# The sums of a sliding-window attention burst: first of 72 small matmuls, or behind 24 of them

## The chip, the core and the metric

The kernel runs on one core of one Trainium2 chip. The metric is the device time of one execution in microseconds (us); where several executions are given, their median counts. A change is measured against runs of the kernel before on the same chip.

## The reference

Two attention blocks read the same input x (2048 rows of 1024) and are mixed by a gate. Block A is linear attention; block B, which the change touches, is a local attention of 32 heads of 32: each position looks at 8 keys, 2 apart, at or before itself.

```python
H = 32; Dh = D // H
W, dil = 8, 2
idx = pos[:, None] - (jnp.arange(W) * dil)[None, :]      # positions looked at
mask = idx >= 0
logits = jnp.einsum("bhsd,bhswd->bhsw", q, kg) * Dh ** -0.5
logits = jnp.where(mask[None, None, :, :], logits, -1e9)
attn = _softmax(logits, axis=-1)
o = jnp.einsum("bhsw,bhswd->bhsd", attn, vg)
b = o_as_rows @ wo
...
return g * a + (1 - g) * b          # g = sigmoid((x * gate_w).sum(-1))
```

The softmax is computed as exponentials of the masked scores, a sum over the keys (the denominator), and a sum of values weighted by the exponentials, divided by the denominator at the end.

## The kernel before

**Stages.** The even and the odd positions are held apart, so that "2 apart" becomes "next to each other". TensorE first makes B's values for all rows (L1405 to L1414), then B's keys and queries (L1507 to L1523), then A's keys, A's state matrix (L1620 to L1643), A's queries and the output (L1688 and on). Each of these is made of groups of 8 or 16 matmuls of 128x128 weights against 512 columns, recorded at L1349, L1628 and L1700.

**The local attention** is cut into 18 fills: 9 for each parity, of 2 x 57 or 2 x 56 queries. They are strewn between the large groups by `slot` (L1493), one fill to five groups or so. A fill (`fill`, L1435) has these operations:

- two DMAs that fetch 2 x 64 rows of values into `vt` (L1441);
- the score burst `s_fn` on TensorE (L1444): 64 small matmuls, 32-row tiles of the array, whose 57 columns each land in the four PSUM banks `SO[0]` to `SO[3]` (banks 4 to 7);
- the exponential on ScalarE into `E` (L1454) and the band mask on VectorE (L1457);
- three slots later (`PVLAG`), the values burst `values` (L1461): in one operation, `each` (L1463), 64 value matmuls and 8 sum matmuls;
- then, for each half, the logarithm of the denominators (L1483), the exponential of its negative (L1484), both on ScalarE, and the product with the weighted values (L1485) on VectorE.

**The values burst.** All 72 matmuls use tiles of 64 rows x 32 columns of the array: the row half h (0 or 1) holds one set of 64 keys, the column quarter j (0 to 3) one of four heads. So there are eight tiles, and the loops over j and h visit them in turn. A value matmul (L1468) has a head's 64 x 32 values as weights and streams 57 columns of E, one head's; it writes `SO[h]`. There are 8 x 4 x 2 = 64, with c from 0 to 7 outermost. A sum matmul (L1474) has a 64 x 32 block of ones as weights and streams 456 columns of E, the eight heads of one j at once; it writes `SO[2 + h]`. There are eight, one on each tile. Every matmul is preceded by a weight load of its own, so the burst is 72 pairs. In the kernel before, the sums stand behind the round c = 2, that is behind 24 value matmuls (`SUMS_AT = 2`, L1251 and L1471).

**What sets the order of the work.** A planner (`Prog`, L63) collects operations with costs and dependencies, lays them out in time by these costs (`schedule`, L122), and `emit` (L207) writes each engine's list. A dependency across engines is a wait on a semaphore ahead of the operation's first instruction; an operation counts its semaphore up once, on the instruction that its function returns, here on `last`, the last value matmul. The order within an operation is that in which its function issues. The planner books the values burst at 0.66 us, whatever stands inside it, and so does not see the order of the 72 pairs.

Of the kernel before, what the change touches and what calls it, by code (L numbers as in the profile page):

```python
# [1119 lines left out]
def build_kernel(nc, A_x, A_wqkv, A_wo, B_x, B_wqkv, B_wo, gate_w, out):  # L1120
# [10 lines left out]
    def SB(shape, dtype, name, at=None):  # L1131
        n = SZ[dtype]
        for d in shape[1:]:
            n *= d
        if at is None:
            at = base[0]
            base[0] += (n + 31) // 32 * 32
        uid[0] += 1
        h = nc.alloc_sbuf_tensor_at("%s_%d" % (name, uid[0]), list(shape), dtype, offset=at)
        return Tile("S", h, at, list(shape), dtype)  # L1140
# [48 lines left out]
    def hb(p0, p1, half):  # L1189
        return [("H%d" % half, p0, p1, None)]  # L1190
# [9 lines left out]
    ones = SB([128, 128], BF16, "ones")  # L1200
# [47 lines left out]

    FILL = 0.2
    PVLAG = 3  # L1250
    SUMS_AT = 2  # L1251
    WARM = 50
    PASSES = 6
    mm = lambda n: max(n / 2400.0, 0.0267) + 0.0025
# [3 lines left out]
    def plan(seen):  # L1258
# [169 lines left out]
        SO = banks[4:8]  # L1428
# [6 lines left out]
        def fill(e_, qs, nq, offs):  # L1435
            t0 = e_ * HS
            k0 = [qs + nq * h - offs[h] for h in range(2)]
            m = msk[KINDS.index((nq, offs))]
            vt, vslot = vr.next()
            for h in range(2):  # L1440
                P.op("sp", lambda e, h=h: e.dma_start(vt[64 * h:64 * h + 64, :], vB_hbm[t0 + k0[h]:t0 + k0[h] + 64, :]), 0.4,  # L1441
                     reads=[hb(t0 + k0[h], t0 + k0[h] + 64, i) for i in range(2)], writes=[vt.all()], chan="v%d_%d" % (vslot, h), lat=0.5)

            def s_fn(e):  # L1444
                for c in range(8):
                    for h in range(2):
                        for j in range(4):
                            last = e.matmul(SO[j].ap(c * nq, (c + 1) * nq)[64 * h:64 * h + 64, :], kT[32 * j:32 * j + 32, c, t0 + k0[h]:t0 + k0[h] + 64],  # L1448
                                            qT[32 * j:32 * j + 32, c, t0 + qs + h * nq:t0 + qs + (h + 1) * nq], start=True, stop=True, tile_position=(32 * j, 64 * h))
                return last  # L1450
            P.op("pe", s_fn, 0.65, mode="r", reads=[kT.part((0, 8), (t0 + k0[0], t0 + k0[1] + 64)), qT.part((0, 8), (t0 + qs, t0 + qs + 2 * nq))],
                 writes=[s.iv for s in SO], name="S")
            E, _ = Er.next()
            P.op("act", lambda e: e.activation(E[:, 0:32 * nq].rearrange("p (j q) -> p j q", j=4), ps[:, 4:8, 0:8 * nq], ACT.Exp), act(32 * nq),  # L1454
                 reads=[s.iv for s in SO], writes=[E.all()])
            ev = lambda: E[:, 0:32 * nq].rearrange("p (g q) -> p g q", g=16)
            mk = P.op("dve", lambda e: e.tensor_tensor(ev(), ev(), m[:, :, :].rearrange("p r q -> p (r q)")[:, None, :].to_broadcast([128, 16, 2 * nq]), ALU.mult),  # L1457
                 0.15 + 32 * nq / 1920.0, reads=[E.all(), m.all()], writes=[E.all()])
            masks.append(mk)

            def values():  # L1461

                def each(e):  # L1463
                    for c in range(8):
                        for j in range(4):
                            for h in range(2):
                                hd = 4 * c + j
                                last = e.matmul(SO[h].ap(c * nq, (c + 1) * nq)[32 * j:32 * j + 32, :], vt[64 * h:64 * h + 64, hd * 32:hd * 32 + 32],  # L1468
                                         E[64 * h:64 * h + 64, (8 * j + c) * nq:(8 * j + c + 1) * nq],
                                         start=True, stop=True, tile_position=(64 * h, 32 * j))  # L1470
                        if c == SUMS_AT:  # L1471
                            for j in range(4):
                                for h in range(2):
                                    e.matmul(SO[2 + h].ap(0, 8 * nq)[32 * j:32 * j + 32, :], ones[64 * h:64 * h + 64, 0:32],  # L1474
                                             E[64 * h:64 * h + 64, 8 * j * nq:8 * (j + 1) * nq],
                                             start=True, stop=True, tile_position=(64 * h, 32 * j))
                    return last
                bi = [s.iv for s in SO]
                P.op("pe", each, 0.66, mode="c", reads=[vt.all(), ones.all(), E.all()], writes=bi, name="PV")
                for g in range(2):  # L1480
                    L, _ = Lr.next()
                    pb = lambda o, g=g: ps[:, 4 + 2 * o:6 + 2 * o, 4 * g * nq:4 * (g + 1) * nq]
                    P.op("act", lambda e, L=L, pb=pb: e.activation(L[:, :, 0:4 * nq], pb(1), ACT.Ln), act(8 * nq), reads=[SO[2].iv, SO[3].iv], writes=[L.all()])  # L1483
                    P.op("act", lambda e, L=L: e.activation(L[:, :, 0:4 * nq], L[:, :, 0:4 * nq], ACT.Exp, scale=-1.0), act(8 * nq), reads=[L.all()], writes=[L.all()])  # L1484
                    P.op("dve", lambda e, L=L, pb=pb, g=g: e.tensor_tensor(  # L1485
                        qT[:, 4 * g:4 * g + 4, t0 + qs:t0 + qs + 2 * nq].rearrange("p c (h q) -> p h c q", h=2),
                        pb(0).rearrange("p h (c q) -> p h c q", c=4), L[:, :, 0:4 * nq].rearrange("p h (c q) -> p h c q", c=4), ALU.mult), dps(8 * nq),
                        reads=[SO[0].iv, SO[1].iv, L.all()], writes=[qT.part((4 * g, 4 * g + 4), (t0 + qs, t0 + qs + 2 * nq))])
            after(PVLAG, values)
# [12 lines left out]
        def after(n, f, cols=False):  # L1502
            later.append((slot_n[0] + n, f, cols))
            later.sort(key=lambda x: x[0])
# [291 lines left out]
def bass_gated_mix__linear_attn_block__sliding_local_dilated__prompt_kernel(nc, A_x, A_wqkv, A_wo, B_x, B_wqkv, B_wo, gate_w, out):  # L1796
    return build_kernel(nc, A_x, A_wqkv, A_wo, B_x, B_wqkv, B_wo, gate_w, out)
# [28 lines left out]
```

## Time and profile before

| | us |
|---|---|
| median of 3 runs | 486.28 (486.14 to 486.35) |
| the profiled execution | 485.35 |
| its span, from the first to the last instruction | 483.5 |
| TensorE matmuls busy | 480.0, 99% |
| VectorE busy | 294.9, 61% |
| ScalarE busy | 146.9, 30% |
| the first values burst, by the chain of work that ended last | 131.24 to 131.96 |

Times inside the profile count from the first instruction. A line such as L1468 is a line of the kernel; PE is TensorE's matmuls and PEld its weight loads, which overlap the matmuls. DVE is VectorE, ACT ScalarE. A timeline row gives the start, the length from the first start to the last end of the instructions that it merges, the engine, line, operation, what is written and read, the tile of the array (64*32), the operand's shape, and the count. Square brackets hold idle time ahead, and who ended it. Matmuls on different tiles overlap, and each lasts longer than its columns stream. The granted TensorE clock was full (1.0) over the whole span.

### The profile page before, as it was taken

The page shows a single profiled execution, that of the slowest core. Times are in us where ns is not written, and L with a number is a line of the kernel's source. Part 1 is how long each engine was busy: PE and PEld are TensorE (multiplying, and loading weights), DVE is VectorE, ACT ScalarE, POOL GpSimd, SP SyncE. Part 2 cuts the span into 40 slices and gives each one's busy share as a digit, 9 for nine tenths or more (in the row PEclk, how much of TensorE's full clock was granted, in tenths as well). Part 3 has the DMA queues.
Part 4 walks back from the last instruction along what each step waited for, and adds up shares of the span by engine and source line. Part 5 has one row for each costly group of instructions (what it writes and reads, how often), then busy time and mean ns, then how long its engine had stood idle before and what let it go on. Part 6 is the DMA issues. An engine that isn't in the chain of part 4 may idle for free.

```text
span 483.5 us, 10963 instructions
## 1 busy us (share of the span) xinstructions
PE 480.0 (99%) x4882; PEld 229.0 (47%) x4882; DVE 294.9 (61%) x490; ACT 146.9 (30%) x229; POOL 39.4 (8%) x40
## 2 busy tenths in 40 slices
PE   9999999999999999999999999999999999999997
PEld 6444444444444444444455555444444444444444
DVE  2212186799777778766733222489987777767522
ACT  2111111112344446666654356264222000011000
POOL 3000000000000000000015757010000000000000
DMA  8999996223100032013004340571234111122111
GB/s 243 203 190 322 340 342 188 81 94 107 26 23 26 25 110 73 27 34 111 24 25 122 129 104 4 132 197 24 65 89 87 45 43 45 44 66 66 45 45 48
DMA packets 73977, 48.51 MB, mean 100 GB/s; under 512 B 38337, under 2 KB 67394, under 8 KB 73922
## 3 DMA queue, kind: packets, MB, share of 16 engines
q1 hardware_dynamic: 73090, 46.94, 35.5%
q10 hardware_dynamic: 832, 0.79, 0.8%
q8 instruction: 40, 0.66, 0.6%
q14 instruction: 15, 0.12, 0.1%
HBM read 30.41 MB, written 8.39 MB: 80 GB/s over the span
## 4 chain that ended last, share of the span: by engine, by line
PE 99%; DVE 0%; issue 0%
PE ps_all L1349 58%; PE ps_all L1700 23%; PE ps_all L1628 12%; PE ps_all L1448 2%; PE ps_all L1468 2%; PE ps_all L1385 1%; PE ps_all L1474 1%; PE ps_all L1607 1%; PE ps_all L1655 0%; DVE o L1379 0%
## 5 line engine op out<-in xcount | busy, mean ns | idle before, releaser
L1349 PE MATMUL ps_all<-w,xT 128*128 128x512 bf16 x512 | 112.9, 379 | 0.0
L1349 PE MATMUL ps_all<-xT,w 128*128 128x512 bf16 x512 | 112.2, 379 | 0.0
L1349 PEld LDWEIGHTS ps_all<-xT,w 128*128 128x128 bf16 x512 | 49.3, 98 | 58.7
L1349 PEld LDWEIGHTS ps_all<-w,xT 128*128 128x128 bf16 x512 | 49.0, 98 | 57.6
L1355 ACT ACTIVATE e<-ps_all 128x512 bf16<-128x512 f32 x64 | 38.2, 597 | 109.5 <-PE ps_all L1349 108.7
L1700 PE MATMUL ps_all<-w,qT 128*128 128x512 bf16 (+1 forms) x264 | 60.7, 373 | 0.0
L1700 PE MATMUL ps_all<-kT,aT 128*128 128x512 bf16 (+1 forms) x264 | 60.7, 373 | 0.0
L1349 PE MATMUL ps_all<-kT,xT 128*128 128x512 bf16 x256 | 57.9, 379 | 0.0
L1628 PE MATMUL ps_all<-pk,xn 128*128 128x512 bf16 x256 | 57.8, 380 | 0.0
L1700 PEld LDWEIGHTS ps_all<-w,qT 128*128 128x128 bf16 x264 | 25.8, 98 | 29.6 <-issue 0.2
L1700 PEld LDWEIGHTS ps_all<-kT,aT 128*128 128x128 bf16 x264 | 25.8, 98 | 29.4
L1349 PEld LDWEIGHTS ps_all<-kT,xT 128*128 128x128 bf16 x256 | 24.7, 98 | 30.0 <-issue 0.7
L1376 DVE CAST vst<-ps_all 128x512 bf16<-128x512 f32 x16 | 11.1, 692 | 45.4 <-PE ps_all L1349 45.4
L1628 PEld LDWEIGHTS ps_all<-pk,xn 128*128 128x128 bf16 x256 | 23.9, 98 | 27.4
L1379 DVE TENSOR_SCALAR o<-ps_all,gm 128x512 bf16<-128x512 f32 (+1 forms) x27 | 19.7, 731 | 28.0 <-PE ps_all L1700 28.0
L1356 DVE TENSOR_SCALAR e<-e 128x512 bf16<-128x512 bf16 x64 | 18.8, 296 | 27.5 <-ACT e L1355 27.2
L1454 ACT ACTIVATE E<-ps_all 128x1824 bf16<-128x1824 f32 (+1 forms) x18 | 30.4, 1688 | 15.8 <-PE ps_all L1448 15.1
L1457 DVE TENSOR_TENSOR E<-E,msk 128x1824 bf16<-128x1824 bf16 (+1 forms) x18 | 19.8, 1103 | 23.3 <-ACT E L1454 23.3
L1590 POOL TENSOR_TENSOR zacc<-zacc,pk 128x1024 f32<-128x1024 f32 x15 | 32.0, 2130 | 16.5 <-DVE E L1457 15.7
L1485 DVE TENSOR_TENSOR qT<-ps_all,L 128x456 bf16<-128x456 f32 (+1 forms) x36 | 21.2, 625 | 19.4 <-ACT L L1484 19.2
L1377 ACT ACTIVATE kT<-ps_all 128x512 bf16<-128x512 f32 x25 | 14.2, 599 | 33.6 <-PE ps_all L1349 33.6
L1377 ACT ACTIVATE vst<-ps_all 128x512 bf16<-128x512 f32 x16 | 9.6, 597 | 48.7 <-PE ps_all L1349 48.7
(63 smaller groups left out, 361.0 us busy)
## 6 DMA issues: line engine op xcount, KB each, us to landing
v<-vB_hbm SPq DMA_DIRECT2D x36, 128.0 KB, 2.6
vB_hbm<-vst SPq DMA_DIRECT2D x32, 128.0 KB, 4.9
w<-in_B_wqkv_dram SPq DMA_DIRECT2D x4, 1024.0 KB, 8.4
xt<-in_A_x_dram SPq DMA_DIRECT2D x16, 256.0 KB, 5.3
w<-in_A_wqkv_dram SPq DMA_DIRECT2D x4, 1024.0 KB, 9.7
xn<-in_A_x_dram SPq DMA_DIRECT2D x8, 512.0 KB, 3.7
out_dram<-o SPq DMA_DIRECT2D x15, 256.0 KB, 2.1
kT<-in_A_wqkv_dram SPq DMA_DIRECT2D x2, 1024.0 KB, 5.6
```

The source lines that it names most:

```text
L1349: last = e.matmul(bank.ap(), lhs(dc), rhs(dc), start=(dc == 0), stop=(dc == 7))
L1355: P.op("act", lambda e: e.activation(e_[:, :], bank.ap(), ACT.Exp), act(512), reads=[bank.iv], writes=[e_.all()])
L1356: P.op("dve", lambda e: e.tensor_scalar(e_[:, :], e_[:, :], 1.0, 1e-6, op0=ALU.min, op1=ALU.add), 0.25, reads=[e_.all()], writes=[e_.all()])
L1376: fd = lambda e: e.tensor_copy(dst, src())
L1377: fa = lambda e: e.activation(dst, src(), ACT.Copy)
L1379: fd = lambda e: e.tensor_scalar(dst, src(), scale, None, op0=ALU.mult)
L1454: P.op("act", lambda e: e.activation(E[:, 0:32 * nq].rearrange("p (j q) -> p j q", j=4), ps[:, 4:8, 0:8 * nq], ACT.Exp), act(32 * nq), rea ...
L1457: mk = P.op("dve", lambda e: e.tensor_tensor(ev(), ev(), m[:, :, :].rearrange("p r q -> p (r q)")[:, None, :].to_broadcast([128, 16, 2 * n ...
L1485: P.op("dve", lambda e, L=L, pb=pb, g=g: e.tensor_tensor(qT[:, 4 * g:4 * g + 4, t0 + qs:t0 + qs + 2 * nq].rearrange("p c (h q) -> p h c q" ...
L1590: P.op("pool", lambda e, t=t: e.tensor_tensor(zacc[:, :], zacc[:, :], pkS[:, t, :], ALU.add), 2.2, reads=[src, zacc.all()], writes=[zacc.a ...
L1628: last = e.matmul(bank.ap(), tl[:, t, cs:cs + 128], pkS[:, t, r * 512:(r + 1) * 512], start=(t == 0), stop=(t == NT - 1))
L1700: last = e.matmul(bank.ap(0, f1 - f0), lh[:, k, t * 128:(t + 1) * 128], w[:, k, f0:f1], start=(first and k == 0), stop=(not first and k == 7))
```

## The change

The loop with the eight sums is moved from behind the round c = 2 to the front of `each`, and the constant that named the place goes. Operands, shapes, tile positions, the number of instructions, the operation's reads and writes and its booked cost stay as they are.

```diff
-    SUMS_AT = 2
...
                 def each(e):
+                    for j in range(4):
+                        for h in range(2):
+                            e.matmul(SO[2 + h].ap(0, 8 * nq)[32 * j:32 * j + 32, :], ones[64 * h:64 * h + 64, 0:32],
+                                     E[64 * h:64 * h + 64, 8 * j * nq:8 * (j + 1) * nq],
+                                     start=True, stop=True, tile_position=(64 * h, 32 * j))
                     for c in range(8):
                         for j in range(4):
                             for h in range(2):
...
                                 last = e.matmul(SO[h].ap(c * nq, (c + 1) * nq)[32 * j:32 * j + 32, :], vt[64 * h:64 * h + 64, hd * 32:hd * 32 + 32],
...
-                        if c == SUMS_AT:
-                            for j in range(4):
-                                for h in range(2):
-                                    e.matmul(SO[2 + h].ap(0, 8 * nq)[32 * j:32 * j + 32, :], ones[64 * h:64 * h + 64, 0:32],
-                                             E[64 * h:64 * h + 64, 8 * j * nq:8 * (j + 1) * nq],
-                                             start=True, stop=True, tile_position=(64 * h, 32 * j))
                     return last
```

## The prediction

> **What bounds the kernel now.** The page comes first: which engine is full, and whether the chain that ends last ever leaves it.
>
> ```profile
> span 483.5 us, 10963 instructions
> PE 480.0 (99%) x4882; PEld 229.0 (47%) x4882; DVE 294.9 (61%) x490; ACT 146.9 (30%) x229; POOL 39.4 (8%) x40
> ...
> PE 99%; DVE 0%; issue 0%
> PE ps_all L1349 58%; PE ps_all L1700 23%; PE ps_all L1628 12%; PE ps_all L1448 2%; PE ps_all L1468 2%; PE ps_all L1385 1%; PE ps_all L1474 1%; PE ps_all L1607 1%; PE ps_all L1655 0%; DVE o L1379 0%
> ```
>
> TensorE is the whole path, so whatever a values burst gains or loses on TensorE is gained or lost in the span. The next view is the chain in order of time around one burst, then the two lines' own groups (duration in ns, min/median/max).
>
> ```profile
> 125.95 5.29 PE ps_all L1349 x24
> 131.24 0.21 PE ps_all L1468 x24
> 131.44 0.19 PE ps_all L1474 x8
> 131.64 0.33 PE ps_all L1468 x40
> 131.96 5.29 PE ps_all L1349 x24
> ```
> ```profile
> L1468 PE MATMUL ps_all<-E,v x1152: 182/194/198, 131.2 to 314.3; 64*32 64x57 bf16 x172, 64*32 64x56 bf16 x20
> L1474 PE MATMUL ps_all<-E,ones x144: 347/350/352, 131.3 to 313.9; 64*32 64x456 bf16 x128, 64*32 64x448 bf16 x16
> ```
>
> A burst is 24 value matmuls, 8 sums, 40 value matmuls, 0.72 us in all, and there are 144 / 8 = 18 bursts. The chain dates pieces by ends, so what limits the burst has to be read from its starts. The timeline of the first burst, weight loads (PEld) and matmuls apart, cut where the loads pause:
>
> ```profile
> 131.16 0.17 PEld L1468 LDWEIGHTS ps_all<-E,v 64*32 64x32 bf16 x24 [0.42 <-DVE mx L1308]
> 131.24 0.11 PEld L1474 LDWEIGHTS ps_all<-E,ones 64*32 64x32 bf16 x8
> 131.29 0.09 PEld L1468 LDWEIGHTS ps_all<-E,v 64*32 64x32 bf16 x1
> 131.16 0.28 PE L1468 MATMUL ps_all<-E,v 64*32 64x57 bf16 x24
> 131.26 0.37 PE L1474 MATMUL ps_all<-E,ones 64*32 64x456 bf16 x8
> ...
> 131.39 0.28 PEld L1468 LDWEIGHTS ps_all<-E,v 64*32 64x32 bf16 x24
> ...
> 131.65 0.21 PEld L1468 LDWEIGHTS ps_all<-E,v 64*32 64x32 bf16 x15
> 131.89 0.10 PEld L1349 LDWEIGHTS ps_all<-xT,w 128*128 128x128 bf16 x1
> ```
>
> Second figure: from the first start to the last end; one load lasts 0.09. So 24 + 8 + 1 = 33 loads and 24 + 8 = 32 matmuls, 65 instructions, start between 131.16 and 131.29, at about 3 ns a pair of load and matmul... and then no load for 0.10 us. From 131.39 loads come steadily: 24 in 0.28 - 0.09 = 0.19 us, 8.3 ns each. The 24th starts at 131.58, and a second hold follows: the next starts at 131.65, 0.06 later instead of 0.008. Fifteen more at the same pace start up to 131.65 + 0.21 - 0.09 = 131.77, and 0.12 later the next group loads. The **pace and the holds of the issue**, not the array, set this burst from 131.29 to 131.77, two thirds of its 0.72 us.
>
> What ends a hold? I look at the single first matmul of the values burst, and of the score burst (L1448), which has 64 small matmuls and no sums:
>
> ```profile
> 131.16 0.20 PE L1468 MATMUL ps_all<-E,v 64*32 64x57 bf16 x1
> ```
> ```profile
> 125.25 0.21 PE L1448 MATMUL ps_all<-qT,kT 32*64 32x57 bf16 x1
> ...
> 125.25 0.23 PEld L1448 LDWEIGHTS ps_all<-qT,kT 32*64 32x64 bf16 x33 [0.42 <-issue]
> ...
> 125.49 0.35 PEld L1448 LDWEIGHTS ps_all<-qT,kT 32*64 32x64 bf16 x31
> 125.88 0.10 PEld L1349 LDWEIGHTS ps_all<-xT,w 128*128 128x128 bf16 x1
> ```
>
> Values: the first matmul ends at 131.16 + 0.20 = 131.36, and load 34 starts 0.03 later. Scores: it ends at 125.25 + 0.21 = 125.46, and load 34 starts 0.03 later, again after exactly 33 loads. The second hold of the values: the 25th matmul is the first sum, 131.26 + 0.35 = 131.61, and the 58th load starts at 131.65, 0.03 to 0.04 later; that is again 65 instructions behind it (matmul 25 is instruction 50, load 58 is instruction 115). The score burst has no long matmul, and its last 31 loads run unbroken: 30 x 8.3 ns + 0.10 = 0.35. The last values burst, 183 us later, does the same (first matmul, then load 34):
>
> ```profile
> 313.74 0.20 PE L1468 MATMUL ps_all<-E,v 64*32 64x56 bf16 x1
> ...
> 313.97 0.09 PEld L1468 LDWEIGHTS ps_all<-E,v 64*32 64x32 bf16 x1
> ```
>
> 313.74 + 0.20 + 0.03 = 313.97. My reading: **at most 65 instructions are under way, and a later one enters 0.03 us after the end of the matmul 65 places ahead**. Every burst starts with a full stock because the group before it takes 5.29 us for 24 matmuls, 0.22 each.
>
> **The change part by part.** Nothing is added or taken away: 72 pairs before and after, the same operands, one count at the end of the operation, the same cost in the planner's books, hence the same order of all operations. No DMA is issued in the burst and nothing passes another queue. Only the place of 8 pairs moves, 24 places ahead, 18 times. Four things follow.
>
> 1. The array. The eight sums now start at 131.16 to 131.19 and stream together for 0.19 (chain row), to 131.36. The 25 pairs behind them that are already under way run then: three rounds of eight took 131.16 to 131.26, 0.10, so they are through by about 131.46. In the kernel before, the sums streamed from 131.26 to 131.45, and the first hold (131.29 to 131.39) lay wholly beside them. That cover goes: the array runs empty behind 131.46 until load 34 arrives.
>
> 2. The first hold. Load 34 waits for the first matmul, which is now a sum. How long does a sum at the head of a burst last? The trace shows none there. Lower end: 0.35, its median in the middle. Upper end: 0.36. The first value matmul lasts 0.20 (198 ns is the maximum of L1468), while the 24th, started just ahead of 131.26 and ended at 131.16 + 0.28 = 131.44, lasts 0.19; so the head costs about 0.01 more. I take 0.36, because the nearest row is the first matmul of this very burst. Load 34 then starts at 131.16 + 0.36 + 0.03 = 131.55 instead of 131.39: 0.36 - 0.20 = **0.16 us later**.
>
> 3. The second hold. Matmul 25 becomes a value matmul, started by 131.46, ended by 131.65; by step 2's pace load 58 comes at 131.55 + 24 x 0.0083 = 131.75, later than 131.65 + 0.03 = 131.68. So the hold of 0.06 becomes a plain 0.008: **0.05 us back**.
>
> 4. The tail. From load 34 to load 72 are 38 steps of 8.3 ns, 0.317: the last load starts at 131.55 + 0.317 = 131.87, against 131.77; in hundredths that is 0.10, by the two holds 0.16 - 0.05 = 0.11, and I keep the latter, since it has fewer rounded ends. The 0.12 to the next group stays; behind the score burst, whose last load starts at 125.49 + 0.25 = 125.74, it is 0.14 without any sum in the burst. It is how a change from small tiles to whole-array weights looks, and the last matmuls are value matmuls in both kernels.
>
> Sum per burst: 0.11 us later. Times 18: **+2.0 us**; with 0.35 for the sum, 0.10 and +1.8. Nothing late on another engine follows: who waits for the burst is the logarithm, and it waits for the last value matmul, not for the sums:
>
> ```profile
> ACT L L1483 <- PE ps_all L1468: 14.5, 18, 2.9
> ```
>
> The operation counts once, on its last instruction, so earlier sums let nobody start earlier; and ACT and DVE, 30% and 61% busy, follow TensorE, which waits for them nowhere in the chain. They are 0.11 late with it, as is every later transfer.
>
> The profiled execution took 485.35 us (its span of 483.5 and 1.85 around it), 0.9 below the median of 486.28. The sum is made on the span: 483.5 + 2.0 = 485.5, so a profiled execution of 487.35. On the median: 486.28 + 2.0 = **488.3 us**.
>
> [...]
>
> **The rivals.** *Issue does not wait for ends: faster.* Place freed at the start of an instruction, or new ones after a fixed time. Load 34 then stays at 131.39, no second hold is left, and the last load comes at 131.39 + 0.317 = 131.71, by the one hold 0.05 earlier: 18 x 0.05 = 0.9 us, 485.4. It decides below a load 34 of 131.44, 0.28 behind the start of the burst. For it: the first hold alone shows only 0.20 against 0.21 of matmul time. Against it: these 0.01 do come back in load 34 (0.23 and 0.24 behind the start), and the second hold has no cause without the first sum's end. 6%.
>
> *The second hold is no sum's.* If it belongs to the place in the code, at the 58th pair, it stays: 0.16 a burst, 18 x 0.16 = 2.9 us, 489.2. For it: it stands at load 58 in every burst I read. Against: the score burst passes its 58th load unbroken. 6%.
>
> *Nothing changes.* If the next group's first load were bound to something older than the last value matmul, such as a wait of its own at 131.89, up to 0.12 of lateness would vanish there: 486.3. Against: the score burst, of another length, shows the same distance of 0.14 behind its last load. 5%. That the edit does nothing to the order is excluded: it moves instructions within one operation.
>
> **How the numbers follow.** Forecast 83%, rivals 6, 6 and 5%. About 0.2%, 1.0 us, is what a measurement of this kernel can tell from no change. Slower by more: the forecast and the second rival, 89%. The first rival's 0.9 us lies just inside the bound, so I split it 2% faster and 4% same; with the 5% of no change that makes 9% same. Range: the forecast's ends, 0.10 and 0.11 a burst, give 488.1 to 488.3; an uncertain pace and drain of 0.02 a burst adds 0.4 to either side, and the medians' own spread of 0.1 stands beside it: 487.6 to 488.8. That holds the forecast's 83% and reaches to no rival.
>
> **What would show it.** In the timeline of the changed kernel: eight sums first, at the start of the burst; their first lasts 0.36; 33 loads, then a hold that ends 0.39 behind the start (right), or 0.23 (first rival). After it 39 loads unbroken at 8.3 ns (right), or broken by 0.06 at the 58th (second rival). The next group's load 0.12 behind the last (right). In the chain, a values burst of 0.83 instead of 0.72, everything else as before. Wrong would be above all a first sum that ends sooner at the head of a burst, or a sequencer that refills while the sums stream.

## The result and the profile after

The change makes the kernel slower: median 488.01 us (487.62 to 488.68, 6 runs) against 486.21 us (485.49 to 486.45, 6 runs) of the kernel before, a ratio of 1.0045 with a 95% interval of 1.0033 to 1.0057. On 486.2 that is 1.6 to 2.8 us, and 2.0 was forecast. The profiled execution took 487.88 us.

In the code after, the sums stand at L1465 and the values at L1472; other lines move up by one or two. The page:

```profile
span 486.1 us, 10898 instructions
PE 475.3 (98%) x4817; PEld 230.0 (47%) x4882; DVE 295.0 (61%) x490; ACT 146.9 (30%) x229; POOL 39.4 (8%) x40
...
PE 98%; issue 2%; DVE 0%
```

TensorE still is the whole path. The new 2% of "issue" is no idle time: there are 4882 weight loads and only 4817 matmuls, so 65 records of matmuls are missing in this trace. In the chain a large group shows 5.13 us for 23 matmuls behind 0.16 of "issue", together the 5.29 that 24 took before. The chain around the second burst:

```profile
143.80 0.32 PE ps_all L1465 x8
144.12 0.52 PE ps_all L1472 x64
144.64 0.16 issue
144.80 5.13 PE ps_all L1348 x23
```

A burst now counts 0.32 + 0.52 = 0.84 us instead of 0.72. Where the 0.12 lie is seen in the timeline of the first burst (start, length, count), loads first:

```profile
131.69 0.11 PEld L1465 LDWEIGHTS ps_all<-E,ones 64*32 64x32 bf16 x8 [0.42 <-DVE mx L1307]
131.72 0.33 PEld L1472 LDWEIGHTS ps_all<-E,v 64*32 64x32 bf16 x25
...
132.09 0.41 PEld L1472 LDWEIGHTS ps_all<-E,v 64*32 64x32 bf16 x39
132.53 0.10 PEld L1348 LDWEIGHTS ps_all<-xT,w 128*128 128x128 bf16 x1
...
131.69 0.39 PE L1465 MATMUL ps_all<-E,ones 64*32 64x456 bf16 x8
131.89 0.27 PE L1472 MATMUL ps_all<-E,v 64*32 64x57 bf16 x24
```

Again 8 + 25 = 33 loads and 8 + 24 = 32 matmuls, then no new load until 132.09, which is 0.40 behind the start of the burst; before it was 0.23. Then 39 loads run unbroken: 0.41 - 0.09 = 0.32 us for 38 steps of 8.3 ns. The 24th value matmul starts at 131.89 + 0.27 - 0.19 = 131.97, so from then on the array has nothing to start for 0.1 us. The sums' own row has the length that the forecast had to guess (ns, min/median/max):

```profile
L1465 PE MATMUL ps_all<-E,ones x144: 359/363/363, 131.7 to 316.3; 64*32 64x456 bf16 x128, 64*32 64x448 bf16 x16
```

131.69 + 0.36 + 0.03 = 132.08 to 132.09: load 34 again enters 0.03 behind the end of the first matmul. The last burst agrees, 0.39 from its start at 316.23 (its sums have 448 columns) to load 34:

```profile
316.23 0.11 PEld L1465 LDWEIGHTS ps_all<-E,ones 64*32 64x32 bf16 x8 [0.42 <-issue]
316.26 0.32 PEld L1472 LDWEIGHTS ps_all<-E,v 64*32 64x32 bf16 x25
...
316.62 0.41 PEld L1472 LDWEIGHTS ps_all<-E,v 64*32 64x32 bf16 x39
```

Below, "burst" means from its first weight load to the next group's first weight load, as a mean over the 18 bursts of a trace: 0.724 us before, 0.839 after. The difference times 18 is 2.08 us. The two profiled spans differ by 2.6, and the rest stands ahead of every burst. The warm-up matmuls of the first rows, before and then after:

```profile
0.84 5.33 PE ps_all L1385 x50
```
```profile
0.84 5.86 PE ps_all L1384 x50
```

0.53 us more until the first real group may start. Two kernels below, with the sums behind 32 and behind 40 values, differ from the one before in a single constant and show 5.30 and 5.83 here, so it is a difference between executions and not the change's.

### The profile page after: what moved, and what is told of

Its sections match the earlier page's. It is cut to its first block, busy times and chain, and to the rows that moved or that the text cites. A ratio compares the mean times of both kernels' runs of the same rounds, so it can differ in the third digit from the quotient of the medians.

```text
span 486.1 us, 10898 instructions
## 1 busy us (share of the span) xinstructions
PE 475.3 (98%) x4817; PEld 230.0 (47%) x4882; DVE 295.0 (61%) x490; ACT 146.9 (30%) x229; POOL 39.4 (8%) x40
## 4 chain that ended last, share of the span: by engine, by line
PE 98%; issue 2%; DVE 0%
PE ps_all L1348 56%; PE ps_all L1698 23%; PE ps_all L1626 11%; PE ps_all L1447 2%; PE ps_all L1472 2%; PE ps_all L1384 1%; PE ps_all L1465 1%; PE ps_all L1605 1%; PE ps_all L1653 0%; DVE o L1378 0%
## 5 line engine op out<-in xcount | busy, mean ns | idle before, releaser
L1348 PE MATMUL ps_all<-w,xT 128*128 128x512 bf16 x493 | 109.5, 379 | 2.4 <-issue 2.1
L1348 PE MATMUL ps_all<-xT,w 128*128 128x512 bf16 x497 | 109.9, 379 | 1.7 <-issue 1.4
L1626 PE MATMUL ps_all<-pk,xn 128*128 128x512 bf16 x242 | 54.9, 379 | 2.1 <-issue 2.1
```

The lines of the kernel that those rows point to most:

```text
L1348: last = e.matmul(bank.ap(), lhs(dc), rhs(dc), start=(dc == 0), stop=(dc == 7))
L1626: last = e.matmul(bank.ap(), tl[:, t, cs:cs + 128], pkS[:, t, r * 512:(r + 1) * 512], start=(t == 0), stop=(t == NT - 1))
```

## The experiments

Theory, as in the prediction, where it is the author's reading of the rows before: at most 65 instructions are under way; the next one enters 0.03 us after the end of the matmul 65 places ahead. In all 18 bursts of the trace before, load 34 starts 0.030 to 0.031 us behind the recorded end of the first matmul. (The first run shows that the count is one too high.) Rival, in most runs: cover, that is, a refill that comes a fixed time after the stock has run out, whatever the matmuls' lengths; sums then only have to stream beside that hold. All kernels start from the one before, except the sixth, which starts from the one after; each ratio is to the kernel before.

**One sum first.** The helpers `val(c, k)` and `tot(k)` issue a value or a sum matmul on tile k = 2j + h; the lines below stand in `each` in place of the two loops.

```diff
...
+                    tot(0)
+                    for c in range(3):
+                        for k in range(1, 8):
+                            val(c, k)
+                    for k in range(1, 5):
+                        val(3, k)
+                    for k in range(1, 8):
+                        tot(k)
+                    rest = [(3, k) for k in range(5, 8)] + [(c, k) for c in range(4, 8) for k in range(1, 8)]
+                    for n, (c, k) in enumerate(rest):
+                        if n % 4 == 0:
+                            val(n // 4, 0)
+                        last = val(c, k)
```

> One sum is the first of the burst, on one tile; the other seven tiles go on with values, and the other seven sums stand at places 27 to 33, where the stock ends. Only the first instruction pair is long. Theory (the next weight load enters 0.03 us after the end of the matmul 65 instructions ahead): load 34 starts 0.39 to 0.40 us behind the start of the burst, as with all eight sums first; 38 steps of 8.3 ns follow; first load to the next group's load 0.84 us against 0.72 before; 18 x 0.115 = 2.1 us slower than before. Rival (cover: the hold comes a fixed 0.10 to 0.13 us after the stock of 65 has run out, whatever the first matmul is): the stock runs out at 0.13, load 34 at 0.23 to 0.26, burst 0.68 to 0.74, so 0.7 us faster to 0.4 us slower than before.

Measured: 489.89 us, ratio 1.0085 (1.0072 to 1.0099); burst 0.948.

```profile
131.67 0.09 PEld L1473 LDWEIGHTS ps_all<-E,ones 64*32 64x32 bf16 x1 [0.42 <-DVE mx L1308]
131.67 0.17 PEld L1467 LDWEIGHTS ps_all<-E,v 64*32 64x32 bf16 x25
131.77 0.12 PEld L1473 LDWEIGHTS ps_all<-E,ones 64*32 64x32 bf16 x7
...
132.06 0.35 PEld L1467 LDWEIGHTS ps_all<-E,v 64*32 64x32 bf16 x32 [0.18 <-issue]
...
132.44 0.14 PEld L1467 LDWEIGHTS ps_all<-E,v 64*32 64x32 bf16 x7
...
131.78 0.62 PE L1473 MATMUL ps_all<-E,ones 64*32 64x456 bf16 x7
```

1 + 25 + 7 = 33 loads are out by 131.77 + 0.12 - 0.09 = 131.80, 0.13 behind the start, as before; still load 34 comes at 132.06, 0.39 behind the start, where the theory has it and the rival (0.23 to 0.26) does not. The burst is longer than either said, by a second hold ahead of the 66th load (32 loads up to 132.06 + 0.35 - 0.09 = 132.32, the next at 132.44). I had the eighth sum as the 33rd matmul, which is instruction 66, one beyond the stock. Its load is among the 33 that are out by 131.80, but the last row shows that it was itself held back with load 34: the last of these seven sums ends at 131.78 + 0.62 = 132.40, so with 0.35 us of its own it started at 132.05. 0.03 to 0.04 behind its end, load 66 comes. The next run tests whether that sum's place is what cost the second hold.

This also corrects the count. Instruction 66 has a weight load 65 places ahead of it, and that load had long ended. Here it is the matmul 32 pairs behind a long one, 64 places, that is held first, to 132.05; the next weight load, 65 places behind, follows it at once, at 132.06.

**One sum first, the others one place earlier.** The edit is shown against the kernel of the last run.

```diff
-                    for k in range(1, 5):
+                    for k in range(1, 4):
                         val(3, k)
...
-                    rest = [(3, k) for k in range(5, 8)] + [(c, k) for c in range(4, 8) for k in range(1, 8)]
+                    rest = [(3, k) for k in range(4, 8)] + [(c, k) for c in range(4, 8) for k in range(1, 8)]
```

> As the run with one sum first, but the other seven sums stand one place earlier, at pairs 26 to 32, so that all of them are within the stock of 65 instructions (33 loads, 32 matmuls). In that run the 33rd matmul was a sum, and the late second hold, at load 66, is 33 pairs behind it. Theory (end of the matmul 65 instructions ahead): load 34 at 0.39 to 0.40 again, no hold at load 66, last load 0.71 to 0.74, burst 0.84 to 0.87; 2.1 to 2.6 us slower than before, and about 1.5 us faster than the first version of this run. Rival (the extra 0.11 us came from the one tile whose eight values were put off, not from the sum): the hold near load 66 stays, burst 0.95, 4.0 us slower than before.

Measured: 487.95 us, ratio 1.0046 (1.0032 to 1.0059); burst 0.840.

```profile
131.42 0.09 PEld L1473 LDWEIGHTS ps_all<-E,ones 64*32 64x32 bf16 x1 [0.42 <-DVE mx L1308]
131.42 0.17 PEld L1467 LDWEIGHTS ps_all<-E,v 64*32 64x32 bf16 x24
131.51 0.11 PEld L1473 LDWEIGHTS ps_all<-E,ones 64*32 64x32 bf16 x7
131.54 0.09 PEld L1467 LDWEIGHTS ps_all<-E,v 64*32 64x32 bf16 x1
...
131.81 0.41 PEld L1467 LDWEIGHTS ps_all<-E,v 64*32 64x32 bf16 x39 [0.18 <-issue]
```

The second hold is gone, the first is where it was: load 34 at 131.81, 0.39 behind the start. A single sum at the head, with the values on seven tiles going on, costs as much as all eight, 0.840 against 0.839. So the refill follows the end of the first matmul, 0.36 long, and not the sums' 0.19 us in the array.

**One round later, and two.** Behind 32 and behind 40 values.

```diff
-    SUMS_AT = 2
+    SUMS_AT = 3
```
```diff
-    SUMS_AT = 2
+    SUMS_AT = 4
```

> The sums one round later than before, behind 32 values. Theory (end of the matmul 65 instructions ahead): load 34 stays at 0.23, the sums start at 0.235 to 0.29 and stream beside nothing; the 67th load (2 x 33 instructions behind the first sum) waits for the first sum's end, 0.235 + 0.35 + 0.03 = 0.62, instead of 0.51 by pace; a hold of about 0.11 there; burst 0.79 to 0.80 against 0.72, so 1.3 us slower than before. Rival (cover: ends hold back nobody; the sums stream 0.235 to 0.425 while loads pile up, then 32 values in four rounds of 0.033): last load 0.55, burst 0.69 to 0.70, 0.5 us faster than before, and no hold at load 67.

Measured: 487.35 us, ratio 1.0035 (1.0021 to 1.0049); burst 0.795, so 1.3 us by the trace.

```profile
131.44 0.14 PEld L1474 LDWEIGHTS ps_all<-E,ones 64*32 64x32 bf16 x7
...
131.63 0.19 PEld L1468 LDWEIGHTS ps_all<-E,v 64*32 64x32 bf16 x17
131.81 0.15 PEld L1468 LDWEIGHTS ps_all<-E,v 64*32 64x32 bf16 x7
132.00 0.10 PEld L1349 LDWEIGHTS ps_all<-xT,w 128*128 128x128 bf16 x1
...
131.43 0.42 PE L1474 MATMUL ps_all<-E,ones 64*32 64x456 bf16 x8
```

The first sum starts at 131.43 and lasts 0.35; 0.03 behind its end, at 131.81, the last seven loads begin. The 17 ahead of them start up to 131.63 + 0.19 - 0.09 = 131.73 (that they begin only at 131.63, 0.20 behind the first sum's start, belongs to the last section). So a hold stands there, ahead of load 66 (the expectation said 67; the first sum is pair 33, and 33 + 33 is 66). The rival, which had this kernel faster than before, falls.

> The sums two rounds later than before, behind 40 values. Theory: the first sum is pair 41, so its end binds only what comes 33 pairs later, behind the burst; no hold by a sum's end is left, but the sums now stream beside nothing (0.29 to 0.48), and the values behind them wait for the array. Burst 0.71 to 0.73, the same as before within 0.2 us of the span. Rival (cover: what counts is that the sums stream during the hold, which they miss by 0.06 us here as much as in the round before it): 0.19 us of the sums uncovered, burst 0.80 or more, 1.4 us slower.

Measured: 486.21 us, ratio 1.0006 (0.9997 to 1.0015); burst 0.724, equal to before. The rival said 0.80.

```profile
131.95 0.15 PEld L1474 LDWEIGHTS ps_all<-E,ones 64*32 64x32 bf16 x8
132.02 0.15 PEld L1468 LDWEIGHTS ps_all<-E,v 64*32 64x32 bf16 x8
...
132.16 0.18 PEld L1468 LDWEIGHTS ps_all<-E,v 64*32 64x32 bf16 x16
132.39 0.10 PEld L1349 LDWEIGHTS ps_all<-xT,w 128*128 128x128 bf16 x1
...
131.96 0.42 PE L1474 MATMUL ps_all<-E,ones 64*32 64x456 bf16 x8
132.16 0.23 PE L1468 MATMUL ps_all<-E,v 64*32 64x57 bf16 x8
```

Here the wait is for the sums' stream: they start from 131.96, and the first value on a sum's tile starts 0.20 later. The last load is out by 132.16 + 0.18 - 0.09 = 132.25, ahead of the first sum's end (131.96 + 0.35 = 132.31), so no sum's end binds anything in this burst any more, and what that saves the uncovered stream takes. Two places that lie one round apart differ by 0.07 us a burst, and the later one is the better; a rule of "as early as possible" does not give that, nor does cover.

**One round, then the sums.** Behind 8 values.

```diff
-    SUMS_AT = 2
+    SUMS_AT = 0
```

> The sums behind 8 values. Theory: load 34 waits for a value matmul and comes at 0.23 as before; the first sum is matmul 9, starts at 0.035, ends at 0.39, and binds load 42 at 0.42 (0.30 by pace), a hold of 0.13 between loads 41 and 42 and none at load 34 beyond the usual; burst 0.79 to 0.80, 18 x 0.075 = 1.35 us slower than before, two thirds of the change's loss. Rival (cover: the hold comes a fixed 0.10 to 0.13 after the stock of 65 has run out, here at 0.28): load 34 at 0.38 to 0.41, burst 0.82 to 0.85, 1.8 to 2.3 us slower.

Measured: 487.52 us, ratio 1.0031 (1.0019 to 1.0042); burst 0.800, 1.4 us by the trace.

```profile
131.67 0.11 PEld L1468 LDWEIGHTS ps_all<-E,v 64*32 64x32 bf16 x8 [0.42 <-DVE mx L1308]
131.70 0.11 PEld L1474 LDWEIGHTS ps_all<-E,ones 64*32 64x32 bf16 x8
131.73 0.11 PEld L1468 LDWEIGHTS ps_all<-E,v 64*32 64x32 bf16 x8
131.91 0.15 PEld L1468 LDWEIGHTS ps_all<-E,v 64*32 64x32 bf16 x17
...
132.09 0.34 PEld L1468 LDWEIGHTS ps_all<-E,v 64*32 64x32 bf16 x31
132.47 0.10 PEld L1349 LDWEIGHTS ps_all<-xT,w 128*128 128x128 bf16 x1
...
131.71 0.38 PE L1474 MATMUL ps_all<-E,ones 64*32 64x456 bf16 x8
```

The hold moves with the first sum: 8 + 8 + 8 + 17 = 41 loads, and load 42 at 132.09, 0.42 behind the start. A miss in a detail: loads 25 to 41 start only at 131.91, when the sums have streamed, so load 34 comes at 0.26 and not at 0.23. They would have had to be a second load ahead on their tiles, which no burst of the traces before and after shows, see the last section.

**Half as many columns.** This starts from the kernel after. It leaves out the denominators of half the heads and uses the other half's twice.

```diff
-                            e.matmul(SO[2 + h].ap(0, 8 * nq)[32 * j:32 * j + 32, :], ones[64 * h:64 * h + 64, 0:32],
-                                     E[64 * h:64 * h + 64, 8 * j * nq:8 * (j + 1) * nq],
+                            e.matmul(SO[2 + h].ap(0, 4 * nq)[32 * j:32 * j + 32, :], ones[64 * h:64 * h + 64, 0:32],
+                                     E[64 * h:64 * h + 64, 8 * j * nq:(8 * j + 4) * nq],
...
-                    pb = lambda o, g=g: ps[:, 4 + 2 * o:6 + 2 * o, 4 * g * nq:4 * (g + 1) * nq]
+                    pb = lambda o, g=g: ps[:, 4 + 2 * o:6 + 2 * o, 4 * g * (1 - o) * nq:(4 * g * (1 - o) + 4) * nq]
```

> All eight sums first, as in the change, but each streams 228 columns instead of 456: the denominators of half the heads are left out, and the other half's are used twice. Theory: the first sum lasts 0.363 - 228/456 x 0.190 = 0.268, so load 34 comes at 0.30 instead of 0.396, the 38 steps behind it are as before, burst 0.745 against 0.84 with whole sums and 0.72 before; 18 x 0.02 = 0.4 us slower than before, 1.7 us faster than the change. Rival (place: whatever stands first with weights of its own delays the refill, its length does not matter): load 34 at 0.39, burst 0.84, 2.1 us slower than before.

Measured: 486.16 us, ratio 1.0005 (0.9996 to 1.0014); burst 0.745.

```profile
131.70 0.11 PEld L1465 LDWEIGHTS ps_all<-E,ones 64*32 64x32 bf16 x8 [0.42 <-DVE mx L1307]
131.73 0.23 PEld L1472 LDWEIGHTS ps_all<-E,v 64*32 64x32 bf16 x25
132.00 0.40 PEld L1472 LDWEIGHTS ps_all<-E,v 64*32 64x32 bf16 x39
...
131.70 0.29 PE L1465 MATMUL ps_all<-E,ones 64*32 64x228 bf16 x8
```

Load 34 at 132.00, 0.30 behind the start, as the theory has it; place alone does not set it. The burst is 0.839 - 0.745 = 0.094 us shorter than in the kernel after, which is the 228 columns left out: 228/456 of 0.19 is 0.095.

**The sums last.** `last` is now the eighth sum, on which the operation counts.

```diff
-    SUMS_AT = 2
+    SUMS_AT = 7
...
-                                    e.matmul(SO[2 + h].ap(0, 8 * nq)[32 * j:32 * j + 32, :], ones[64 * h:64 * h + 64, 0:32],
+                                    last = e.matmul(SO[2 + h].ap(0, 8 * nq)[32 * j:32 * j + 32, :], ones[64 * h:64 * h + 64, 0:32],
```

> The sums last, behind all 64 values. Theory: load 34 at 0.23, no hold behind it, last load at 0.23 + 0.317 = 0.55; no later load of this burst waits for a sum, but the next group of 128x128 weights comes a fixed time ahead of the end of the last matmul (0.07: a value matmul of 0.195 that starts with the last load, next load 0.127 behind it), now a sum that ends at 0.55 + 0.35 = 0.90; next load at 0.83, burst 0.83, 1.9 us slower than before. Rival (the next group's load follows the last load of the burst by a fixed 0.127, whatever that matmul's length): burst 0.675, 0.9 us faster than before.

Measured: 487.92 us, ratio 1.0041 (1.0028 to 1.0055); burst 0.839.

```profile
131.62 0.22 PEld L1468 LDWEIGHTS ps_all<-E,v 64*32 64x32 bf16 x33 [0.42 <-DVE mx L1308]
...
131.85 0.34 PEld L1468 LDWEIGHTS ps_all<-E,v 64*32 64x32 bf16 x31
132.11 0.15 PEld L1474 LDWEIGHTS ps_all<-E,ones 64*32 64x32 bf16 x8
132.46 0.10 PEld L1349 LDWEIGHTS ps_all<-xT,w 128*128 128x128 bf16 x1 [0.20 <-issue]
...
132.12 0.42 PE L1474 MATMUL ps_all<-E,ones 64*32 64x456 bf16 x8
```

All 72 loads are out by 132.11 + 0.15 - 0.09 = 132.17, 0.55 behind the start, the fastest issue of all these kernels. But the last sum ends at 132.12 + 0.42 = 132.54, and the next group's load comes 0.07 to 0.08 ahead of that, 0.29 behind the last load and not 0.127. The end of the burst costs what its front has saved.

No place tried here beats the kernel before: the bursts are 0.839 (first), 0.800 (behind 8), 0.724 (behind 24, before), 0.795 (32), 0.724 (40) and 0.839 us (last).

## Why the prediction was right, point by point

- **The array (step 1).** Right. The sums stream at once, the pairs behind them are through 0.28 behind the start of the burst (forecast about 0.30), and the array then has nothing to start until load 34. Only the 25th of these pairs was not through: its load was out, and its matmul was held until load 34.
- **The first hold (step 2).** Right in mechanism and nearly in size: the first sum lasts 0.363 (0.36 taken), and load 34 comes 0.396 behind the start against 0.39. One sum first, half the columns and one round ahead shift it as the first sum's end says. A refill a fixed 0.10 to 0.13 us after the stock has run out would fit the kernel after and half the columns, but fails with one sum first (0.26) and with the sums behind 8 values, where load 34 follows without a pause. The runs can't tell what inside the chip frees the place; they show only that it is tied to that matmul's recorded end, which the profile models.
- **The second hold (step 3).** Right: 39 loads unbroken after it. That it belongs to the first sum and not to the 58th pair, the second rival, is shown by its moving to load 42 with the sums behind 8 values and to load 66 with the sums behind 32.
- **The tail (step 4).** Right: 0.127 from the last load to the next group's, in both kernels. The third rival's absorption did not occur.
- **The sum.** 0.11 us a burst forecast, 0.116 measured; 2.0 us against 2.08 by the trace and 1.6 to 2.8 by the runs. The time of 488.3 lies 0.3 above the measured median, which is less than single runs of one kernel differ.

One count of step 2 is wrong without harm: 65 is one too high, as the first run showed. The kernel after shows it too:

```profile
131.89 0.37 PE L1472 MATMUL ps_all<-E,v 64*32 64x57 bf16 x25
```

The 25th value, matmul 33, starts at 131.89 + 0.37 - 0.18 = 132.08, just ahead of load 34, though its own load was out by 131.96. In the 36 bursts of the traces before and after, the least distance in a burst from a matmul's end to the start of the matmul 32 pairs behind it is 0.026 to 0.027 us, and to the start of the load 33 pairs behind it 0.030 to 0.032. The sum is untouched, since the forecast used only the distance to the load. Whether 64 instructions or 32 matmuls are counted stays open, since every matmul has a load of its own.

One more reading falls: that any matmul which has ended makes room. With one sum first, load 34 came 0.26 us behind load 33, although the first value matmuls, begun at 131.67 and 0.19 to 0.20 long, had ended by 131.87, 0.19 ahead of it.

## What to carry to other kernels

In a burst of many small matmuls with a load each, ask of each long one which pair stands 32 behind it: in the bursts before and after, its matmul started no sooner than 0.026 us after the long one's end, and the next load no sooner than 0.030. In the bursts tried here, the long matmuls were cheap behind 24 values, where the pairs 32 behind them were late anyway from the first hold (the second took 0.06), and behind 40, where these belong to the next group (0.724 us a burst both times); they were dear as the first of a burst (0.839), and dear as the last (0.839), where the next group's load came only 0.07 to 0.08 us ahead of the last sum's end. Whether the same places and distances hold in another kernel was not shown. Read such a burst from the starts of its weight loads, cut where they pause, since the chain by ends shows only sums.

## What the runs showed beyond that

In the 36 bursts of the traces before and after, weight loads run one ahead on each tile and no further: none starts before the matmul ahead of it on its tile has started, and the least distance between the two starts is 0.001 us. In the kernel after, the loads of the first eight values start at once behind those of the sums, while the sums stream on the same tiles; the next 17 wait until the first values start at 131.89:

```profile
131.72 0.11 PEld L1472 LDWEIGHTS ps_all<-E,v 64*32 64x32 bf16 x8
...
131.90 0.15 PEld L1472 LDWEIGHTS ps_all<-E,v 64*32 64x32 bf16 x17
```

The next group's first load comes at a like distance ahead of the recorded end of a burst's last matmul, whether that is a value of 0.195 us (0.071 to 0.072 in all bursts of the kernels before and after) or a sum of 0.36 (0.07 to 0.08 in the first burst with the sums last).
